# A state-space convolution and an MLP on one core: five chunks of channels instead of six, outer products spread over four PSUM banks, and target times for each chunk

## The chip, the core and the metric

The kernel runs on one core of one Trainium2 chip. The metric is the device time of one execution in microseconds (us); the time before is the median of three runs, 1096.41 us (1095.74 to 1097.32). The trace is that of one further execution, whose span from the first to the last instruction is 1094.6 us.

## The reference, cut to what matters

Two computations share one normalised input and are multiplied at the end. The first is a long convolution for each of 576 channels: its kernel K is a sum over 128 complex exponentials, and the convolution goes through a Fourier transform of twice the length. The second is an MLP with a hidden width of 4608.

```python
xn = layernorm(u)                                  # (2048, 576)
P  = exp((A * dt[:, None])[:, :, None] * arange(2048))
K  = 2.0 * einsum("dn,dnl->dl", C, P).real         # (576, 2048), 128 terms each
s  = irfft(rfft(xn.T, 4096) * rfft(K, 4096))[:, :2048].T + xn * D_skip
h  = gelu(layernorm(xn) @ w1 + b1)                 # (2048, 4608)
g  = silu(h @ w2 + b2)
out = u + s * g
```

## The kernel before, in words

**The MLP is the frame.** The loop over `slot` (48 of them: 12 groups of 384 hidden columns, two blocks of 512 tokens, and all of that once more for the second 1024 tokens) issues TensorE work in a fixed order: three pieces of layer 1 (`layer1`, L633, 14 matmuls of 512 columns each), then eight pieces of layer 2 (`layer2`, L707, 72 matmuls of 288 columns). fp32 products are made of three fp32r products of high and low parts, so each hidden tile goes PE, then ScalarE twice (`gelu` L671, `high` L674), then VectorE (`low` L677, which writes `hl`), and layer 2 takes as its third matmul the one that reads `hl`. The stream of PE instructions of a slot is layer 1, layer 2, layer 1 of the next slot, and so on.

**The convolution rides in the gaps of that order.** Channels are worked through in six chunks of `CH` = 96, and a chunk is a chain of visits to PE: `x1` (first transform of the input, L1157, two pieces of 48 channels), `k1` (the same of the kernel K, L1188, two pieces), four times `s2` (second transform, L1217), after each two of them an `inverse` (L1260), and at the end `i1` (L1286), whose result goes to DRAM as `s_s`. Between the visits VectorE and ScalarE transpose, multiply and copy. All visits but the MLP's own use one PSUM tile name, `cv`: two tiles of two banks each. The intermediate spectrum sits in one large tile, `A2` (`A2F` is its flat view).

**K is made by outer products.** 36 blocks of `SB` = 16 channels each go through `tables` (VectorE and ScalarE: phases from `par`, sine and cosine, magnitudes `mg`, weights) and then through `kgen` (L1042, one PE visit of 32 matmuls). The 30 parameters of a channel come in one DMA for each block, `load_par` (L944), into a tile `par` with two buffers. A `kgen` visit can stand alone, or `ride`: it is then issued right ahead of the matmuls of a convolution visit, into the columns from 384 on of the same PSUM banks, which a chunk of 96 leaves empty.

**The order is written by a planner.** `Order` runs when the program is built. It keeps a clock for each engine from estimated durations, has a list of `lines` of steps, and emits a step when its inputs are due and it does not push a step with a due time (`by`) back. Engines run strictly in the order emitted. `pe_turns` decides when a convolution visit comes: `pace` spreads the 48 visits of `c1` evenly up to `END`, `ALONE` and `DUE` hold back a `kgen` that would stand alone, and `HOLD` swaps single steps by hand. When a convolution visit stands at the edge of a slot, `pair` (L616) may go ahead of it: it does two narrow matmuls side by side in place of two of the 42 matmuls of layer 1, for which a second copy of `XR` has been loaded into `bias2` (`load_pair`).

**The beginning.** Sixteen blocks of 128 tokens are normalised. `second(t)` (L456) writes the rows of layer 1's input; for the second eight of them it does so on VectorE into a tile `row`, of which there are four buffers (`NROW`), and two DMAs on SP's queue (L459) store each of them to `y_s`. `norms` is called for blocks 8 to 11 and for 12 to 15, and emits the four `second` steps of a call nearly one behind the other. The names below: row 8 to row 15 for these eight.

Of the kernel before, what the change touches and what calls it, by code (L numbers as in the profile page):

```python
# [18 lines left out]
P = 128  # L19
# [3 lines left out]
CH = 96  # L23
NCH = D // CH
# [5 lines left out]
NPAR = 30  # L30
PK = 144
# [5 lines left out]


# [186 lines left out]
def mixer_kernel(ctx, tc, u, log_a_real, a_imag, c_real, c_imag, log_dt, d_skip, w1, b1, w2, b2,  # L225
# [24 lines left out]
    par_s = dr.tile([P, D, NPAR], F32, name="par_s")  # L250
# [10 lines left out]
    def ys_tile():  # L261
        return sb.tile([P, 2, 2, 2, CH], F32, name="ys", bufs=2)

    idp = sb.tile([P, 4, P], F32, name="f2t")[:, 0]
    f1t = sb.tile([P, 2, 2, 64], F32, name="f1t")
# [13 lines left out]
    def load_consts(g):  # L279
        if g == 0:  # L280
            m = sb.tile([P, 2, 2, CH], F32, name="kk").rearrange("p a b c -> p (a b c)")
# [8 lines left out]
        for k, t in ((ri, TMP["g"]), (1 - ri, TMP["s"])):  # L290
            nc.gpsimd.dma_start(t[r], g1[64 * k + 32 * h:64 * k + 32 * h + 32, 32 * h:32 * h + 32])
        nc.gpsimd.dma_start(dsk[32 * g:32 * g + 1, :].rearrange("p (c m) -> p c m", m=12),
                            dram(d_skip, 12 * g, [[0, 1], [48, D // 48], [1, 12]]))
# [78 lines left out]

    A2 = sb.tile([P, 16, 2, CH, 2], F32, name="A2")
    A2F = A2.rearrange("p a b c r -> p (a b c r)")

# [27 lines left out]
    def norms(b0, n):  # L403
# [49 lines left out]
        def second(t):  # L453
            mv, rs = MV[b0]
            y = sb.tile([P, D], F32, name="row", bufs=NROW)
# [21 lines left out]
    def y_turn(tb, kb):  # L477
# [5 lines left out]
        def load():  # L483
            T.append(sb.tile([P, D], F32, name="row", bufs=NROW)[:, :TB])
# [4 lines left out]
        def turn():  # L489
            T.append(sb.tile([P, D], F32, name="row", bufs=NROW)[:, :TB])  # L490
            nc.vector.transpose(T[1][:n], T[0][:n])

# [250 lines left out]
    def combine_load(b, n, c0, c1):  # L743
        m = c1 - c0
        r = [sb.tile([P, D], F32, name="row", bufs=NROW)[:, :n * m].rearrange("p (i d) -> p i d", i=n) for _ in range(3)]
# [28 lines left out]
    def load_identity():  # L774
        m = sb.tile([P, 32, 24], F32R, name="xc", bufs=NXC).rearrange("p b d -> p (b d)")
        lo = sb.tile([P, 2, 4 * CH], F32R, name="pr").rearrange("p t c -> p (t c)")[:, :D]
        raw = sb.tile([P, 2, 3, CH], F32, name="kk").rearrange("p a b c -> p (a b c)")[:, :P]
# [11 lines left out]
    def finish(b, c0, c1, silu, second_queue, z=None, store=(0, 0), flush=False,  # L789
# [7 lines left out]
        def act_z():  # L797
            if n < D:
                T.append(sb.tile([P, TB], F32, name="h32", bufs=2)[:, :n])
            else:  # L800
                T.append(sb.tile([P, D], F32, name="row", bufs=NROW))
# [33 lines left out]
    def params():  # L835

        nrm, th, ph = (A2F[:, k * D:(k + 1) * D] for k in range(3))
        cr = sb.tile([P, NT, 48], F32, name="xc", bufs=NXC).rearrange("p a b -> p (a b)")[:, :D]
# [5 lines left out]
        dt = ys_tile().rearrange("p i a b c -> p (i a b c)")[:, :D]  # L844
        PRM = [flat(sb.tile([P, 12, 64], F32, name="kt", bufs=2)) for _ in range(2)]
        PRM += [flat(sb.tile([P, 2, 4 * CH], F32, name="pr")), flat(sb.tile([P, SB, NM], F32, name="mg"))]
# [63 lines left out]
        def pack(i):  # L910
            s = slice(i * PK, (i + 1) * PK)

            def columns():
                if i == 0:
                    V.memset(pt[:, :, E1:E1 + 17:8], 1.0)
# [901 lines left out]
```

## Time and profile before

| | |
|---|---|
| time, median of three runs | 1096.41 us (1095.74 to 1097.32) |
| span of the profiled execution | 1094.6 us |
| TensorE (PE) | 1087.5 us busy, 99% |
| VectorE (DVE) | 891.6 us busy, 81% |
| ScalarE (ACT) | 727.4 us busy, 66% |
| GpSimd (POOL) | 188.3 us busy, 17% |
| granted TensorE clock, mean | 0.999 |

PE is counted busy from a matmul's start to its modelled end, and matmuls overlap, so the length of a visit is read from its first start to the start of what follows it. SP's rows tell when its queue issues a DMA; "to landing" is the time from the start of the issue to the semaphore of that DMA.

### The profile page before, as it was taken

To read this page: it belongs to the slowest core of one execution; us is meant where nothing else is said; L and a number is where in the kernel's file an instruction comes from. 1 tells how busy PE (TensorE), PEld (TensorE's weight loads), DVE (VectorE), ACT (ScalarE), POOL (GpSimd) and SP (SyncE) were. 2 spreads that over 40 slices of the span, in tenths; PEclk is the share of its full clock that TensorE was granted. 3 is DMA by queue.
4 is the path that set the end of the run, shared out by engine and by line. 5 is a ranking of instruction groups with operands and counts; after the bars stand their busy time and mean duration, and the time that the engine had idled before them with its cause. 6 is when DMAs were issued, how large, how long until landed. Compare 5 with 4: busy or idle time off the path is not lost.

```text
span 1094.6 us, 27052 instructions
## 1 busy us (share of the span) xinstructions
PE 1087.5 (99%) x11445; PEld 954.1 (87%) x11445; DVE 891.6 (81%) x1302; ACT 727.4 (66%) x1113; POOL 188.3 (17%) x261
## 2 busy tenths in 40 slices
PE   9999999999999999999999999999999999999998
PEld 7989899899888898888988888888888888888897
DVE  7698667889998879889899987997979888766367
ACT  6585699778676674777767848685675757534333
POOL 4566210153010100001100000000001021101132
PEclk9999999999999999999999999999999999999999
DMA  8846663626354152355624216133152434455454
GB/s 226 241 141 160 227 240 137 181 78 156 120 161 139 44 112 66 91 111 147 166 47 119 78 56 141 34 122 87 54 126 44 143 101 132 116 168 151 136 151 102
DMA packets 139554, 138.22 MB, mean 126 GB/s; under 512 B 88953, under 2 KB 105017, under 8 KB 138857
## 3 DMA queue, kind: packets, MB, share of 16 engines
q1 hardware_dynamic: 124424, 85.05, 29.4%
q0 software_dynamic: 14528, 50.71, 15.1%
q8 instruction: 89, 1.46, 0.6%
q10 hardware_dynamic: 480, 0.74, 0.3%
q14 instruction: 33, 0.26, 0.1%
HBM read 102.17 MB, written 36.63 MB: 127 GB/s over the span
## 4 chain that ended last, share of the span: by engine, by line
PE 95%; DMA 2%; DVE 1%; SPq 1%; issue 0%; ACT 0%; DVEq 0%
PE mxb L707 20%; PE mxa L707 20%; PE mxa L633 20%; PE mxb L633 20%; PE cv L1042 3%; PE cv L1217 3%; PE cv L1260 2%; PE cv L1286 2%; PE cv L1188 1%; PE cv L1157 1%; SPq L856 1%; DMA w<-in_A_u_dram 1%; DMA acc<-in_A_u_dram 0%; DMA h<-in_B_b_dram 0%; DVE st L423 0%; DMA raw<-in_B_w_dram 0%
## 5 line engine op out<-in xcount | busy, mean ns | idle before, releaser
L677 DVE TENSOR_TENSOR hl<-h,hh 128x512 fp32r<-128x512 f32 x144 | 98.4, 686 | 96.4 <-ACT hh L674 95.4
L707 PE MATMUL mxa<-w2h,hh 128*128 128x288 f32 x573 | 170.3, 297 | 0.0
L707 PE MATMUL mxb<-w2h,hh 128*128 128x288 f32 x573 | 170.2, 297 | 0.0
L707 PE MATMUL mxb<-w2h,hl 128*128 128x288 f32 x573 | 169.3, 296 | 0.2 <-DVE hl L677 0.2
L707 PE MATMUL mxa<-w2h,hl 128*128 128x288 f32 x573 | 169.1, 295 | 0.0
L707 PE MATMUL mxa<-w2l,hh 128*128 128x288 f32 x573 | 168.6, 294 | 0.0
L707 PE MATMUL mxb<-w2l,hh 128*128 128x288 f32 x573 | 168.6, 294 | 0.0
L671 ACT ACTIVATE h<-mxa,b1t 128x512 f32<-128x512 f32 x73 | 50.0, 687 | 99.2 <-PE mxa L633 97.8
L707 PEld LDWEIGHTS mxa<-w2h,hh 128*128 128x128 f32 x573 | 107.6, 188 | 5.9 <-issue 3.0
L707 PEld LDWEIGHTS mxb<-w2h,hh 128*128 128x128 f32 x573 | 107.6, 188 | 4.3 <-issue 1.7
L707 PEld LDWEIGHTS mxb<-w2l,hh 128*128 128x128 f32 x573 | 107.6, 188 | 0.8
L707 PEld LDWEIGHTS mxa<-w2l,hh 128*128 128x128 f32 x573 | 107.6, 188 | 0.6
L707 PEld LDWEIGHTS mxb<-w2h,hl 128*128 128x128 f32 x573 | 107.5, 188 | 0.5 <-DVE hl L677 0.4
L707 PEld LDWEIGHTS mxa<-w2h,hl 128*128 128x128 f32 x573 | 107.5, 188 | 0.0
L671 ACT ACTIVATE h<-mxb,b1t 128x512 f32<-128x512 f32 x71 | 48.8, 687 | 68.6 <-PE mxb L633 66.2
L674 ACT ACTIVATE hh<-h 128x512 fp32r<-128x512 f32 x144 | 90.7, 631 | 3.7
L944 POOL DMA_DIRECT2D par<-par_s x36 | 27.8, 773 | 367.8 <-DVE mg L988 324.8
L717 DVE TENSOR_TENSOR acc<-mxa,acc 128x576 f32<-128x576 f32 x87 | 65.4, 752 | 26.4 <-PE mxa L707 26.1
L717 DVE TENSOR_TENSOR acc<-mxb,acc 128x576 f32<-128x576 f32 (+1 forms) x89 | 65.8, 741 | 17.8 <-PE mxb L707 17.6
L633 PE MATMUL mxa<-XH,w1h 128*128 128x512 f32 x284 | 79.4, 401 | 0.0
L633 PE MATMUL mxb<-XH,w1h 128*128 128x512 f32 x280 | 77.6, 399 | 0.0
L633 PE MATMUL mxa<-XL,w1h 128*128 128x512 f32 x284 | 76.2, 390 | 0.0
(277 smaller groups left out, 2494.0 us busy)
## 6 DMA issues: line engine op xcount, KB each, us to landing
raw<-in_B_w_dram SPq DMA_DIRECT2D x72, 288.0 KB, 3.4
raw<-in_B_w_dram SPq DMA_DIRECT2D x96, 192.0 KB, 3.6
par_s<-A POOLq DMA_DIRECT2D x4, 2160.0 KB, 8.1
par<-par_s POOLq DMA_DIRECT2D x36, 240.0 KB, 3.7
f2t<-f2q SPq DMA_DIRECT2D x24, 256.0 KB, 3.7
g2t<-g2p SPq DMA_DIRECT2D x24, 256.0 KB, 4.3
bias<-XR SPq DMA_DIRECT2D x42, 128.0 KB, 3.6
raw<-in_B_w_dram SPq DMA_DIRECT2D x48, 96.0 KB, 3.8
```

The source lines that it names most:

```text
L633: nc.tensor.matmul(q, a, b, start=j == 0 and i not in BEGUN, stop=j == len(ops) - 1, skip_group_check=True)
L671: nc.scalar.activation(t, q, AF.Gelu_apprx_tanh, bias=b1t[:, k:k + 1], scale=1.0)
L674: LAST[0] = nc.scalar.activation(hh[:, i], t, AF.Copy)
L677: nc.vector.tensor_sub(hl[:, i], t, hh[:, i].bitcast(F32))
L707: nc.tensor.matmul(q[:, dh, :288], a[:, i, c], b[:, i, d], start=i == 0 and k == 0 and alone != 1, stop=i == G - 1 and k == 2, skip_group_ ...
L717: nc.vector.tensor_add(o, q[:, dh:dh + n, :288], b)
L856: nc.sync.dma_start(r[32 * g:32 * g + 32].rearrange("c (b n) -> c b n", n=32), dram(src[k], 32 * g, [[N, 32], [32 * N, D // 32], [1, 32]]))
L944: nc.gpsimd.dma_start(PAR[b].rearrange("p (g i) k -> p g (i k)", g=4), dram(par_s, (b // 3 * 48 + b % 3 * 4) * NPAR, [[D * NPAR, P], [12 * ...
L1042: nc.tensor.matmul(q[32 * g:32 * g + 32, i // 2, i % 2 * 64:i % 2 * 64 + 64], U[:, ri, 4 * g + i, :], v[:, ri, 4 * g + i, :], start=ri == ...
L1217: nc.tensor.matmul(Q[i][32 * q:32 * q + 32, f, ri::2], m[r, 4 * i + q, 32 * ri:32 * ri + 32], A2[r, 4 * p + 2 * i + q // 2, :, :, q % 2], ...
L1260: nc.tensor.matmul(QI[q // 2][64 * f:64 * f + 64, q % 2, i], MAT["g2t", p + i // 2][r, i % 2, f, ri], YS[p + i // 2][0][r, i % 2, ri, f], ...
L1286: nc.tensor.matmul(Q[h][64 * y:64 * y + 64, t], g1t.rearrange("p a e -> p (a e)"), A2[:, k:k + 2, 1].rearrange("p i d r -> p i r d"), star ...
```

## The change

**Chunks.** The 576 channels go in chunks of 112, 112, 112, 112 and 128. A chunk of 112 has two pieces of 56 for `x1` and `k1`, that of 128 has 48, 48 and 32. Every tile whose size hung on `CH` gets the size of the largest chunk, and views of what a chunk needs. A block of 16 channels can now lie across two pieces, so its parameters come in one or two DMAs (`slots`, `load_table`).

**Outer products.** A chunk of 112 leaves 64 columns of a bank empty, not 128, so a riding `kgen` writes 64 columns in each of the host's four banks and is copied out in two pieces, not one. In the last chunk, which fills a bank, only `x1` and `k1` take riders.

**Memory.** Wider tiles take room, and it is found in three places. The `row` buffers shrink from 576 to 512 columns and the normalised rows move into `A2F`, at the places of `ROWS_AT`: four for the first eight rows, two for rows 8 to 15. The tile `mg` goes, and the magnitudes move to the end of `A2F` (the last four blocks, which meet the chunk of 128, use other tiles). `par` has one buffer, not two, without the two phase columns, which come by a DMA of their own into `pha` (two buffers). The parts of the first transform's matrix are made once and kept in DRAM (`fp_s`), and loaded for each later chunk, where they were made anew.

**The planner.** `pace` gives way to `due`: each visit has a target time between the `BEGIN` of its chunk and the next, by the shares of `PART`; a visit waits longer for a rider that is not ready (`WAITS`). `ALONE` falls from 20 to 1.5, `HOLD` is emptied, and in the last eleven slots no second copy of `XR` is loaded, so no `pair` stands there.

```diff
-CH = 96
-NCH = D // CH
+CHS = 112, 112, 112, 112, 128
+PIECES = ((56, 56),) * 4 + ((48, 48, 32),)
...
-            y = sb.tile([P, D], F32, name="row", bufs=NROW)
+            at = ROWS_AT[(b0 + t) % 4 if b0 < 8 else 4 + t % 2]
+            y = A2F[:, at:at + D]
...
+    ROWS_AT = 4032, 4608, 5184, 6048, 6048, 7200
...
-        PAR[b] = sb.tile([P, SB, NPAR], F32, name="par", bufs=2)
...
+        PHA[b] = sb.tile([P, SB, NPH], F32, name="pha", bufs=2)
+        load_table(PHA[b], ph_s, b, NPH)
...
+        PAR[b] = sb.tile([P, SB, NPAR - NPH], F32, name="par")
+        load_table(PAR[b], par_s, b, NPAR - NPH)
...
-        return ([step(None, 10.0 if b < 6 else 4.5, lambda: load_par(b), mark=("par", b), need=[("pack", b * SB // PK)]
-                      + ([("mags", b - 2)] if b > 1 else [("xn", k) for k in range(8, NT)])),
+        lead = 10.0 if b < 6 else 4.5
...
+                [step(None, lead, lambda: load_par(b), mark=("par", b), need=[pk] + ([("mags", b - 1)] if b else [("xn", k) for k in range(8, NT)]))])
...
-            q = (bank2("cv") if tile is None else tile)[:, :, 384:]
-            Q.append(q)
+                q = [tiles[j // 2][:, j % 2, 448:] for j in range(SB // 4)]
+                Q.extend([(j, 2, tiles[j // 2][:, :, 448:]) for j in (0, 2)])
...
-    HOLD = {("weigh", 19, 3): 1, ("phase", 19): 1, ("frac", 18): 2, ("k", 2, 1): (2, 1), (2, 0, 24): 1, (2, 1, 24): 1, ("k1", 2, 1, 2): 1}
+    HOLD = {}
...
-    END = 1000.0
-    EDGE = 0.2, 0.6
-    ALONE, DUE = 20.0, (160.0, 950.0)
+    BEGIN = 240.0, 400.0, 574.0, 720.0, 880.0, 989.0
+    PART = 0.0, 0.09, 0.18, 0.283, 0.373, 0.469, 0.533, 0.673, 0.833
+    WAITS = 0.5, 28.2
+    ALONE, DUE = 1.5, (164.0, 851.0)
...
-                    elif 1 < k < 2 * NG - 1 and ("acc", slot - k + 1, 3) in od.marks:
+                    elif 1 < k < 2 * NG - 1 and slot < NSLOT - 11 and ("acc", slot - k + 1, 3) in od.marks:
```

The first place to look at is VectorE's order near the beginning, at rows 8 to 11 (`row<-w` before, `A_84<-w` now; `hl` is the MLP's low part, and a name in brackets is a semaphore waited for, DMAHW that of a transfer on SP's queue). Before:

```order
L456 TENSOR_SCALAR row<-w,mv,rs 128x576 [waits DVE_49]
L583 TENSOR_TENSOR w2l<-raw,w2h 128x576 [waits DMAHW1_49,Activation_49]
L583 TENSOR_TENSOR w2l<-raw,w2h 128x576 [waits DMAHW2_49,Activation_49]
L583 TENSOR_TENSOR w2l<-raw,w2h 128x576 [waits DMAHW3_49,Activation_49]
L876 TENSOR_TENSOR kt<-kt,pr 128x576 [waits Activation_49]
L456 TENSOR_SCALAR row<-w,mv,rs 128x576 x3
L677 TENSOR_TENSOR hl<-h_700,hh 128x512 [waits Activation_49]
```

And the same place now:

```order
L494 TENSOR_SCALAR A_84<-w,mv,rs 128x576 [waits DVE_49]
L621 TENSOR_TENSOR w2l<-raw,w2h 128x576 [waits DMAHW1_49,Activation_49]
L621 TENSOR_TENSOR w2l<-raw,w2h 128x576 [waits DMAHW2_49,Activation_49]
L621 TENSOR_TENSOR w2l<-raw,w2h 128x576 [waits DMAHW3_49,Activation_49]
L914 TENSOR_TENSOR kt<-kt,pr 128x576 [waits Activation_49]
L494 TENSOR_SCALAR A_84<-w,mv,rs 128x576
L494 TENSOR_SCALAR A_84<-w,mv,rs 128x576 [waits DMAHW5_49,DMAHW4_49,DVE_49] x2
L715 TENSOR_TENSOR hl<-h_692,hh 128x512 [waits Activation_49]
```

Nothing moved, but rows 10 and 11 now each wait for two transfers: row 10 takes the place of row 8 and waits for row 8's two stores, row 11 for row 9's.

The second place is VectorE's order at rows 12 to 15, where before each row waited for the store of four rows earlier:

```order
L451 RECIPROCAL rs<-rs 128x8 [waits Activation_49]
L456 TENSOR_SCALAR row<-w,mv,rs 128x576 [waits DMAHW5_49,DMAHW4_49,DVE_49]
L456 TENSOR_SCALAR row<-w,mv,rs 128x576 [waits DMAHW5_49,DMAHW4_49]
L456 TENSOR_SCALAR row<-w,mv,rs 128x576 [waits DMAHW7_49,DMAHW6_49]
L456 TENSOR_SCALAR row<-w,mv,rs 128x576 [waits DMAHW1_49,DMAHW0_49]
L677 TENSOR_TENSOR hl<-h_924,hh 128x512 [waits Activation_49,Pool_49]
```

Now:

```order
L488 RECIPROCAL rs<-rs 128x8 [waits Activation_49]
L494 TENSOR_SCALAR A_84<-w,mv,rs 128x576 [waits DMAHW7_49,DMAHW6_49,DVE_49]
L494 TENSOR_SCALAR A_84<-w,mv,rs 128x576 [waits DMAHW1_49,DMAHW0_49]
L494 TENSOR_SCALAR A_84<-w,mv,rs 128x576 [waits DMAHW4_49,DMAHW3_49,DVE_49]
L494 TENSOR_SCALAR A_84<-w,mv,rs 128x576 [waits DMAHW6_49,DMAHW5_49,DVE_49]
L715 TENSOR_TENSOR hl<-h_912,hh 128x512 [waits Activation_49,Pool_49]
```

Here rows 14 and 15 wait for the stores of rows 12 and 13, which stand two steps ahead of them; `hl` stands behind all four as before.

The third place is PE's order in the first chunk, between layer 1 pieces (`mxa`, `mxb` are the MLP's banks). Before, a rider (L1042) and its host `s2` (L1217):

```order
L633 MATMUL mxb<-XL,w1h 128x512 x4
L633 MATMUL mxb<-XH,w1l 128x512 x4
L633 MATMUL mxb<-XR,w1r 128x512
L633 MATMUL mxb<-XR,w1s 128x512
L1042 MATMUL cv<-w 32x64 x32
L1217 MATMUL cv<-A_83,f2t 32x2x96 x32
L633 MATMUL mxa<-XH,w1h 128x512 x4
```

Now, at a place a slot or two later, the outer product (L1112) stands alone and `s2` (L1312) follows one layer 1 piece on:

```order
L671 MATMUL mxb<-XR,w1r 128x512
L671 MATMUL mxb<-XR,w1s 128x512
L1112 MATMUL cv<-w 32x64 x32
L671 MATMUL mxa<-XH,w1h 128x512 x4
L671 MATMUL mxa<-XL,w1h 128x512 x4
L671 MATMUL mxa<-XH,w1l 128x512 x4
L671 MATMUL mxa<-XR,w1r 128x512
L1312 MATMUL cv<-A_84,f2t 32x2x112 x32
```

Over the whole program the rows of PE's order count 66 convolution visits before and 57 now, 36 `kgen` in both, of which 8 stood alone before and 17 now, and 16 `pair` before and 9 now. The number of places at which the MLP's stream is interrupted is 74 in both.

More of the change, by code (lines that the diff above doesn't have):

```diff
@@ L22 @@
 TWO_PI = 6.283185
-CH = 96
-NCH = D // CH
+CHS = 112, 112, 112, 112, 128
+NCH = len(CHS)
+C0 = [sum(CHS[:c]) for c in range(NCH)]
+PIECES = ((56, 56),) * 4 + ((48, 48, 32),)
+CHM = max(CHS)
 SB = 16
@@ L30 @@
 NPAR = 30
+NPH = 2
+LATE_MAG = 32
 PK = 144
@@ L36, with piece_at, slots @@
 TB = 512
+def piece_at(c, i):
+    return C0[c] + sum(PIECES[c][:i])
+def slots(b):
+    c = max(c for c in range(NCH) if C0[c] <= b * SB)
+    k, i0, res = (b * SB - C0[c]) // 4, 0, []
+    for i, m in enumerate(PIECES[c]):
+        n = min(SB // 4 - i0, m // 4 - k)
+        if 0 <= k and n > 0:
+            res.append((c, i, k, i0, n))
+            i0, k = i0 + n, 0
+        else:
+            k -= m // 4
+        if i0 == SB // 4:
+            break
+    return res
 def dve(n):
```

326 lines of the change are left out of this document (197 added, 129 removed).

## Prediction

> **What bounds the kernel now.** The page comes first: which engine is full, and whether the chain that ended last runs through it.
>
> ```profile
> span 1094.6 us, 27052 instructions
> PE 1087.5 (99%) x11445; PEld 954.1 (87%) x11445; DVE 891.6 (81%) x1302; ACT 727.4 (66%) x1113; POOL 188.3 (17%) x261
> PE 95%; DMA 2%; DVE 1%; SPq 1%; issue 0%; ACT 0%; DVEq 0%
> PE mxb L707 20%; PE mxa L707 20%; PE mxa L633 20%; PE mxb L633 20%; PE cv L1042 3%; PE cv L1217 3%; PE cv L1260 2%; PE cv L1286 2%; PE cv L1188 1%; PE cv L1157 1%; SPq L856 1%; DMA w<-in_A_u_dram 1%; DMA acc<-in_A_u_dram 0%; DMA h<-in_B_b_dram 0%; DVE st L423 0%; DMA raw<-in_B_w_dram 0%
> ```
>
> PE is the bound nearly from end to end. So the time changes by two things only: the length of PE's stream of work, and the gaps in it. The convolution (the `cv` lines) is 13% of the chain, the MLP about 80%, which the change leaves as it is. Next, the counts of the convolution's records by form (each matmul of these forms leaves two records, so a visit of `s2` has 64, of `inverse` 128, of `i1` 16):
>
> ```profile
> L1042 PE MATMUL cv<-w 128*32 128x64 f32 x2304 | 39.7, 220 | 0.0
> L1217 PE MATMUL cv<-A,f2t 64*32 64x192 f32 x1536 | 38.7, 333 | 0.0
> L1260 PE MATMUL cv<-ys,g2t 32*64 32x96 f32 x1536 | 22.0, 253 | 0.0
> L1286 PE MATMUL cv<-A,g1t 128*64 128x384 f32 x96 | 17.6, 506 | 0.0
> ```
>
> That is 36 outer products, 24 `s2`, 12 `inverse` and 6 `i1`. Their busy times overlap with their neighbours', so I take the length of a visit from PE's timeline, from its first start to the next start (start, length, then what ran):
>
> ```profile
> 302.35 1.07 PE L633 MATMUL mxa<-XH,w1h 128*128 128x512 f32 x4
> ...
> 305.30 0.39 PE L633 MATMUL mxa<-XR,w1s 128*128 128x512 f32 x1
> ...
> 308.56 1.10 PE L1042 MATMUL cv<-w 128*32 128x64 f32 x64
> 309.60 1.62 PE L1217 MATMUL cv<-A,f2t 64*32 64x192 f32 x64
> 311.15 0.40 PE L707 MATMUL mxa<-w2h,hh 128*128 128x288 f32 x1
> 311.39 0.30 PE L707 MATMUL mxa<-w2l,hh 128*128 128x288 f32 x1
> ...
> 320.66 0.29 PE L707 MATMUL mxb<-w2h,hl 128*128 128x288 f32 x1
> 320.88 0.50 PE L616 MATMUL mxa<-XR,w1s 64*128 64x512 f32 x1
> ...
> 321.31 1.83 PE L1260 MATMUL cv<-ys,g2t 32*64 32x96 f32 x128
> 323.07 1.21 PE L633 MATMUL mxa<-XH,w1h 128*128 128x512 f32 x4
> ```
>
> An outer product takes 309.60 - 308.56 = 1.04 us, `s2` 1.55, `inverse` 1.76, a `pair` 0.43. A matmul of 512 columns takes (305.30 - 302.35)/13 = 0.227 us, one of 288 columns (320.66 - 311.39)/70 = 0.1324, so a column costs 0.0946/224 = 0.00042 us.
>
> ```profile
> 368.93 2.92 PE L1286 MATMUL cv<-A,g1t 128*64 128x384 f32 x16
> 371.78 0.73 PE L633 MATMUL mxa<-XH,w1h 128*128 128x512 f32 x2
> ```
>
> ```profile
> 403.64 0.62 PE L1157 MATMUL cv<-pr,f2t 64*128 64x384 f32 x4
> ...
> 404.89 0.40 PE L707 MATMUL mxa<-w2h,hh 128*128 128x288 f32 x1
> ```
>
> ```profile
> 426.64 0.63 PE L1188 MATMUL cv<-pr,f2t 32*128 32x384 f32 x8
> ...
> 427.91 0.40 PE L707 MATMUL mxb<-w2h,hh 128*128 128x288 f32 x1
> ```
>
> `i1` takes 2.85, `x1` 1.25, `k1` 1.27.
>
> **Part 1, the visits: 4.1 us off PE's stream.** The number of columns over all chunks stays the same, so only what a visit costs beside its columns can be saved. In `x1`, 12 matmuls run two by two: 6 x 384 x 0.00042 = 0.97 of its 1.25 us are columns, 0.28 are not. I take 0.28 for every form and scale the rest by the width.
> - `x1`: 1.41 us with 56 channels, 1.25 with 48, 0.93 with 32. Before 12 x 1.25 = 15.0, now 8 x 1.41 + 2 x 1.25 + 0.93 = 14.7: -0.3.
> - `k1`: the same widths give 1.43, 1.27 and 0.94; 15.2 against 14.9: -0.3.
> - `s2`: 1.55 becomes 1.76 at 112 and 1.97 at 128. Before 24 x 1.55 = 37.2, now 16 x 1.76 + 4 x 1.97 = 36.0: -1.2.
> - `i1`: 2.85 becomes 3.28 and 3.71. Before 17.1, now 16.8: -0.3.
> - `inverse`: its 128 records of 96 columns are the same column work as 64 of 192 in `s2`, and both spread over eight parts of the array, yet it takes 1.76 against 1.55. So 0.2 us of it are neither columns nor the common 0.28, and a chunk of 112, for which `s2` gives 1.76, still fits. At 128 I take `s2`'s 1.97. Before 12 x 1.76 = 21.1, now 8 x 1.76 + 2 x 1.97 = 18.0: -3.1. The bounds are 10 x 1.76 = 17.6 and, all of it beyond 0.28 scaled, 8 x 2.01 + 2 x 2.25 = 20.6.
> - `pair`: 16 before, 9 now. Each one gone brings two matmuls of 512 columns back: 7 x (0.454 - 0.43) = +0.2. Before an `x1` a `pair` also shortens what follows, and five stood so before, one now; with that I take +1.0.
> - Outer products: 36 in both, 1.04 each whether alone or riding. That a rider now writes four banks could change it; I take zero, within -0.1 and +0.1 for each of 19 riders.
> - Interruptions of the MLP's stream: 74 in both: zero.
>
> The sum is -4.2; the rows' rounding is a tenth each, and I take -4.1. The inverse is most of it. On it the Trainium skill's page TensorEngine Tiling (Instruction Overhead) speaks against the change: a matmul has about 60 cycles of overhead that hide below 60 columns, so one of 96 columns should already pay for each column. By that rule the sum is -1.5 instead of -4.1.
>
> **Part 2, the rows at the beginning: 7 us of gaps.** Rows 8 to 15 alternate between two places in `A2F`, where four buffers took them before, and a row can only be written when the store of the row two ahead has landed. VectorE works in order, so behind a waiting row stand the normalisation's statistics and, one to three steps on, the MLP's `hl`, for which PE waits. VectorE's timeline at rows 9 to 11, then PE's third matmul of the layer 2 that follows:
>
> ```profile
> 60.04 1.89 DVE L456 TENSOR_SCALAR row<-w,mv,rs 128x576 f32<-128x576 f32 x3
> 61.85 0.68 DVE L677 TENSOR_TENSOR hl<-h,hh 128x512 fp32r<-128x512 f32 x1
> ...
> 63.42 0.64 DVE L677 TENSOR_TENSOR hl<-h,hh 128x512 fp32r<-128x512 f32 x1
> ...
> 65.44 0.67 DVE L677 TENSOR_TENSOR hl<-h,hh 128x512 fp32r<-128x512 f32 x1
> ```
>
> ```profile
> 64.00 0.29 PE L707 MATMUL mxa<-w2h,hl 128*128 128x288 f32 x1
> ```
>
> The slack is small: `hl` of the first hidden tile ends at 62.5, PE takes it at 64.0. SP's timeline, and the landing of the two stores issued between 61.9 and 62.6, those of row 9:
>
> ```profile
> 57.00 1.14 SPq L459 DMA_DIRECT2D y_s<-row  x2
> 58.25 1.97 SPq L553 DMA_DIRECT2D raw<-in_B_w_dram  x4
> 60.26 1.14 SPq L556 DMA_DIRECT2D raw<-in_B_w_dram  x2
> ```
>
> ```profile
> L459 SPq DMA_DIRECT2D y_s<-row x2: 496/544/592, 61.9 to 62.5; - x2
> DMA to landing us min/median/max: 4.2/4.2/4.2
> ```
>
> Row 8's store is issued at 57.0, long enough before row 10. Row 9 is done at 60.6, but SP is busy with weight loads and issues its store at 61.9 and 62.5; it lands at 62.5 + 4.2 = 66.7. Row 11, which began at about 61.3, now begins there, and `hl`, half a microsecond behind, at 67.3, 5.4 late, ends at 67.9. PE, wanting it at 64.0, stands for 3.9 us. The next `hl` begins 1.57 later as before (two statistics stand between) and ends at 69.5; PE has three matmuls until it wants that one, at 68.3: 1.1 more. The third ends at 71.5, when PE, fifteen matmuls on, gets there: nothing. The first place costs 5.0 us. Nothing hides it: VectorE has no idle time before the row, and before the change rows 10 and 11 waited for no transfer.
>
> That landing stood behind weight loads in flight. Stores at rows 12 to 15 are quicker:
>
> ```profile
> L459 SPq DMA_DIRECT2D y_s<-row x5: 465/541/596, 79.5 to 82.0; - x5
> DMA to landing us min/median/max: 2.1/2.1/2.1
> ```
>
> With 2.1 us in place of 4.2 the first place costs 2.9; that is the lower bound, and I take 5.0, since SP's order and the loads ahead are the same. The Trainium skill's page DMA: Bandwidth & Descriptors (Anatomy of one DMA) gives a fixed 2.0 us and 1 us for each 436 KB: 2.3 us by its figures for a store of 144 KB, an estimate that would put the first place at 3.1 and the time 1.9 us lower; the quiet rows agree with it, the row of row 9, behind other traffic, does not.
>
> ```profile
> 78.90 2.39 DVE L456 TENSOR_SCALAR row<-w,mv,rs 128x576 f32<-128x576 f32 x4
> 81.21 1.28 DVE L677 TENSOR_TENSOR hl<-h,hh 128x512 fp32r<-128x512 f32 x2
> ```
>
> ```profile
> 83.09 0.29 PE L707 MATMUL mxb<-w2h,hl 128*128 128x288 f32 x1
> ```
>
> The second place, in the times of before: row 12 ends at 79.5, its stores go out at 79.5 and 80.1 and land at 82.2; row 14 starts there, 2.2 late. Row 13's go out at 80.7 and 81.3 and land at 83.4; row 15 starts there, and `hl` begins at 84.0, not 81.2, and ends at 84.6, for PE at 83.1: 1.5 us, and 0.2 at the next `hl`. VectorE arrives there 5.4 us late from the first place and PE 5.0, which adds 0.3. I take 2.0, between 1 and 2.5. Both gaps together are 7.0, between 3.9 and 7.5.
>
> **Part 3, the rest of the order: 1 us, between 0 and 4.** `par` has one buffer, so its load can start only when the last reader of the block before is done, and the planner allows 4.5 us from there. The transfer's landing before:
>
> ```profile
> DMA to landing us min/median/max: 3.1/3.7/11.2
> ```
>
> The median fits, the slower ones don't, and VectorE then stands at the magnitudes with `hl` behind it. Two buffers hid this. For 36 blocks, most with other work in between, I take 1 us of PE gaps; `HOLD`, emptied, is in it. More DMA issues on POOL (a second one for each block, at 0.75 us) hide in the 83% of the span in which POOL is idle. A gain here is excluded: PE had no gaps to lose. The end of the kernel stays: at least as many MLP matmuls stand behind the last `i1` in PE's order as before.
>
> **The sum.** Span 1094.6 - 4.1 + 7.0 + 1.0 = 1098.5; the median lies 1.8 us above the span, so 1100.3 us.
>
> **Rivals.**
> - *The stores are in time* (other side). Place: row 11 and rows 14, 15. If row 9's store lands by about 62.9, `hl` ends by 64.0 and the first gap is gone; with the second gone too the time is 1096.4 - 4.1 = 1092.3, up to 1093.3 with part 3. It decides at gaps below 1.9 us in all. For it: two rows of slack are enough when SP is free (row 8's store is). Against it: the store of row 9 isn't even issued before 61.9. With forms that cost by the count and not by columns (`s2` unchanged at 1.55 would take 5 us more off) the sign would turn too; against that, 64 records take 1.04 us with 64 columns and 1.55 with 192. Together 0.13.
> - *About even.* The landing is near its quick value, gaps of 3.9 and nothing in part 3: 1096.4 - 4.1 + 3.9 = 1096.2, up to 1098.6. 0.24.
> - *The inverse pays for each column.* Its upper bound of 20.6 us holds, the gain falls by 2.6, and the time is 1102.9. For it: nothing in the trace shows the visit at another width. Against it: `s2` does the same column work in 0.2 us less. 0.05. It is what the Trainium skill's page TensorEngine Tiling says under Instruction Overhead.
> - *More gaps.* The single `par` buffer stalls VectorE at ten blocks or more by half a microsecond and PE with it, 5 us where I took 1: 1104 to 1106. For it: the landing of up to 11.2. Against it: half of them at 3.7 and less. 0.08.
>
> **How the numbers follow.** The forecast, 1098.6 to 1103, has 0.50. The range of 8 in 10 reaches from 1094.8, inside the even case, to 1105.0. A measurement of this kernel tells about 0.2%, 2.2 us, from no change. Faster than that is the first rival, 0.13; within it the second, 0.24; slower the forecast and the last two rivals, 0.63.
>
> **What would show it.** Right: in the changed profile PE's visits of 1.76 us for `s2` and `inverse` at 112 channels, a wait of PE for `hl` of about 4 us near 64 us and of 1 to 2 us near 88 us, and VectorE idle ahead of L494, released by a DMA to `y_s`. Part 1 is wrong if `inverse` takes 2.0 us, part 2 if VectorE writes rows 9 to 11 without idle time, part 3 if PE's waits after 100 us come to more than 4 us. The prediction falls if PE's stream is shorter by over 6 us or its gaps in the first 100 us stay below 2.

## The result and the profile after

| | before | after |
|---|---|---|
| median | 1096.08 us (1095.45 to 1097.32) | 1108.05 us (1107.62 to 1109.43) |
| profiled execution: time, span | 1096.4, 1094.6 us | 1109.43, 1107.6 us |
| granted TensorE clock, mean | 0.999 | 0.994 |

The ratio is 1.0111, 95% interval 1.0098 to 1.0123. The kernel is slower by 12.0 us where 3.9 were forecast, and 3.0 us outside the range. The direction and the place of the largest loss were right. The sizes were not, and three of the causes are not in the prediction at all. The profiled execution is the slowest of the four after, 1.4 us above their median, and the account below is of that one.

The page after shows it in the chain of work that ended last: PE's share falls from 95% to 89%, and VectorE, transfers and SP's queue take 8% of it where they took 4%.

```profile
span 1107.6 us, 25929 instructions
...
PE 1089.8 (98%) x10881; PEld 949.4 (86%) x10881; DVE 889.1 (80%) x1278; ACT 719.7 (65%) x1101; POOL 226.3 (20%) x316
...
PE 89%; DMA 3%; DVE 3%; SPq 2%; ACT 1%; issue 1%; DVEq 0%
```

To place the 13.0 us of span I took PE's timeline of both kernels and summed two things: the length of each visit, and the excess of each step from one MLP matmul's start to the next over the usual 0.227 us (layer 1) or 0.133 us (layer 2). The "end" is the time from the last matmul's start to the end of the span.

| term | forecast | trace |
|---|---|---|
| visits: `x1` +0.2, `k1` -0.2, `s2` -0.8, `inverse` -1.9, `i1` -0.2; fewer `pair` +0.5 | -4.1 | -2.3 |
| 60 to 100 us, the rows | +7.0 | +8.3 |
| other steps: 480 to 520 us 2.9, 300 us 0.5, 40 to 60 us 0.5 | +1.0 | +3.8 |
| the end | 0 | +3.1 |
| sum | +3.9 | +12.9 |

**The rows.** VectorE's timeline after, at rows 9, 10 and 11 (in brackets: idle time ahead, and who ended it):

```profile
60.55 1.40 DVE L494 TENSOR_SCALAR A<-w,mv,rs 128x576 f32<-128x576 f32 x2
66.69 0.58 DVE L494 TENSOR_SCALAR A<-w,mv,rs 128x576 f32<-128x576 f32 x1 [4.74 <-DMA y_s<-A]
67.18 0.69 DVE L715 TENSOR_TENSOR hl<-h,hh 128x512 fp32r<-128x512 f32 x1
```

Row 11 waits 4.74 us for row 9's store and starts at 66.69 us; the forecast had 66.7. PE's timeline at the `hl` behind it:

```profile
64.30 0.29 PE L745 MATMUL mxa<-w2h,hh 128*128 128x288 f32 x1
64.43 0.29 PE L745 MATMUL mxa<-w2l,hh 128*128 128x288 f32 x1
67.93 0.61 PE L745 MATMUL mxa<-w2h,hl 128*128 128x288 f32 x1 [3.21 <-DVE hl L715]
68.33 0.44 PE L745 MATMUL mxa<-w2h,hh 128*128 128x288 f32 x1
69.45 0.61 PE L745 MATMUL mxa<-w2h,hl 128*128 128x288 f32 x1 [0.44 <-DVE hl L715]
...
74.42 0.45 PE L745 MATMUL mxb<-w2l,hh 128*128 128x288 f32 x1
...
75.11 0.29 PE L745 MATMUL mxb<-w2h,hl 128*128 128x288 f32 x1
```

PE resumes at 67.93 us, as forecast (67.9). Then comes what was not: until 74.7 us the starts stand 0.240 us apart, not 0.133, and a matmul takes 0.44 us instead of 0.29. The busy time by windows has the reason in the seventh column, the granted clock:

```profile
64.43:67.90 3.47, 0.28 (x3) 0.06 (x1) 1.21 (x3) 0.00 (x0) 1.04 (x2) 1.00 0.68 262
67.94:74.77 6.83, 6.39 (x25) 6.04 (x26) 4.80 (x13) 6.71 (x13) 2.95 (x3) 0.50 0.21 65
74.80:84.00 9.20, 9.20 (x62) 8.64 (x61) 9.10 (x13) 7.92 (x21) 3.48 (x3) 1.00 0.17 64
```

For 6.83 us behind the gap TensorE ran at half its clock. Of the 7.0 us of excess between 60 and 80 us, 4.0 are waiting and 3.0 are slow steps. The second place, at 90 us, cost 1.3.

**The switch to the second 1024 tokens.** At 487 us PE waits for `hl` again, and VectorE's waits between 478 and 492 us say for what VectorE stood: the row loads (`row<-y_s`) that the MLP's next input is made from.

```profile
487.17 0.29 PE L745 MATMUL mxb<-w2l,hh 128*128 128x288 f32 x1
489.22 0.40 PE L745 MATMUL mxb<-w2h,hl 128*128 128x288 f32 x1 [1.75 <-DVE hl L715]
```

```profile
DVE row L529 <- DMA row<-y_s: 3.8, 2, 2.8
```

SP's own waits between 430 and 500 us (queue and line, then what ended the wait, us in all) say why they came late: ahead of them in SP's queue stood a load of `f2t` that may only start when the last `k1` has read the tile. SP's timeline has the first row loads, before and after:

```profile
SPq L1182 <- PE cv L1283: 23.3, 1, 23.3
```

```profile
470.31 7.84 SPq L486 DMA_DIRECT2D row<-y_s  x12
```

```profile
480.50 7.72 SPq L524 DMA_DIRECT2D row<-y_s  x12
```

**The end.** The last matmul starts at 1089.13 us before and 1099.03 after, so the span ends 5.5 us behind it before and 8.6 after. POOL's last instruction, a DRAIN at the program's end, is where it goes (its three durations, shortest, median and longest, in ns; before, then after):

```profile
L1813 POOLq DRAIN  x3: 46/103/4467, 1088.4 to 1094.3; - x3
```

```profile
L1919 POOLq DRAIN  x3: 46/103/7175, 1099.6 to 1107.3; - x3
```

It takes 7.2 us instead of 4.5, and it starts 0.6 us behind the last matmul's start instead of 0.7 ahead of it, since VectorE and POOL were still busy with the last step that combines convolution and gate (on VectorE at 1093.7 us after, at 1078.8 before).

**The visits.** Visits of `inverse` at 112 and at 128 channels, and of `s2` at 112, each with the row that follows:

```profile
401.53 1.96 PE L1355 MATMUL cv<-ys,g2t 32*64 32x112 f32 x128
403.43 1.20 PE L671 MATMUL mxa<-XH,w1h 128*128 128x512 f32 x4
```

```profile
983.48 2.10 PE L1355 MATMUL cv<-ys,g2t 32*64 32x128 f32 x128
985.50 0.40 PE L745 MATMUL mxa<-w2h,hh 128*128 128x288 f32 x1
```

```profile
485.16 1.85 PE L1312 MATMUL cv<-A,f2t 64*32 64x224 f32 x64
486.93 0.40 PE L745 MATMUL mxb<-w2h,hh 128*128 128x288 f32 x1
```

`s2` takes 1.77 us, as forecast. `inverse` takes 1.90 and 2.02 where 1.76 and 1.97 were forecast: from 96 channels on it pays 0.13 us for each 16, where `s2` pays 0.22 (1.55 to 1.77).

### The profile page after: what moved, and what is told of

Its sections match the earlier page's. It is cut to its first block, busy times and chain, and to the rows that moved or that the text cites. A ratio compares the mean times of both kernels' runs of the same rounds, so it can differ in the third digit from the quotient of the medians.

```text
span 1107.6 us, 25929 instructions
## 1 busy us (share of the span) xinstructions
PE 1089.8 (98%) x10881; PEld 949.4 (86%) x10881; DVE 889.1 (80%) x1278; ACT 719.7 (65%) x1101; POOL 226.3 (20%) x316
## 4 chain that ended last, share of the span: by engine, by line
PE 89%; DMA 3%; DVE 3%; SPq 2%; ACT 1%; issue 1%; DVEq 0%
PE mxa L745 20%; PE mxb L745 19%; PE mxb L671 19%; PE mxa L671 18%; PE cv L1112 3%; PE cv L1312 3%; PE cv L1355 2%; DMA raw<-in_B_w_dram 2%; PE cv L1381 2%; PE cv L1251 1%; PE cv L1283 1%; SPq L894 1%; DMA w<-in_A_u_dram 1%; DMA y_s<-A 1%; DMA acc<-in_A_u_dram 0%
## 5 line engine op out<-in xcount | busy, mean ns | idle before, releaser
L981 POOL DMA_DIRECT2D par<-par_s x40 | 30.2, 757 | 487.9 <-DVE A L1049 429.4
```

The costliest lines, as they stand in the source:

```text
L981: nc.gpsimd.dma_start(x.rearrange("p (g i) k -> p g (i k)", g=4)[:, :, i0 * n:(i0 + m) * n], dram(t, (piece_at(c, i) + k) * n, [[D * n, P] ...
```

## The experiments

The theory to be tested: four separate causes, namely the rows' two places with the halved clock behind the gap, SP's queue at the switch, the combine steps together with POOL's drain at the end, and an `inverse` that is dearer than forecast. The chief rivals: the clock falls for another reason than PE's idleness, the gaps after 100 us come of the single `par` buffer as the prediction had it, and the end is long by chance. Differences to the changed kernel are differences of medians taken at different times; the kernel before, run beside every experiment, lay between 1095.3 and 1095.8 us there and at 1096.1 beside the changed kernel, so they are good to about 0.8 us.

### Three places for the rows

```diff
-            at = ROWS_AT[(b0 + t) % 4 if b0 < 8 else 4 + t % 2]
-            y = A2F[:, at:at + D]
+            at = ROWS_AT[(b0 + t) % 4 if b0 < 8 else 4 + (b0 + t) % 3 % 2]
+            y = sb.tile([P, 6 * CHM], F32, name="kk")[:, :D] if b0 >= 8 and (b0 + t) % 3 == 2 else A2F[:, at:at + D]
```

> The changed kernel, with three places in turn for rows 8 to 15 instead of two (the third is the tile kk, which nothing else uses so early), so that row 11 waits for row 8's store and no longer for row 9's. Theory A (the rows' stores make the gaps near 64 and 90 us, and the halved clock that follows the first one is its consequence): the excess of PE's steps between 60 and 100 us, 8.3 us in the changed kernel, falls below 1.5 us, the granted clock stays at 1.00 from 50 to 100 us, and the time falls by 7 to 8.5 us, to 1099.5 to 1101. Rival B (the slow clock near 70 us comes of something else, the load on the chip at that time for instance): PE's gaps go, but the clock still halves for 7 us; 4 to 5 us, to about 1103.5. Rival C (VectorE is late there for another reason, the gap only moves): under 2 us.

Measured: 1100.71 us, ratio to before 1.0051 (1.0037 to 1.0065), 7.3 us less than the changed kernel. The busy time by windows:

```profile
60.00:70.00 10.00, 10.00 (x67) 9.42 (x66) 9.79 (x21) 6.77 (x11) 8.40 (x8) 1.00 0.73 247
```

PE is busy through 60 to 70 us, the clock stays at 1.00, and the excess between 60 and 100 us is about 1 us instead of 8.3 (0.7 of it a wait of ScalarE's making at 79 us). The rows were the cause of both the wait and the slow clock. The gap at the switch is still there in this run (1.6 us idle at 478 us), so it is a matter of its own.

### The wait filled with idle work

```diff
+        fill = lambda z: [nc.tensor.matmul(z[:, 0], hh[:, 0, :P], hh[:, 0], start=True, stop=True, skip_group_check=True)
+                          for _ in range(16)]
...
+                (turn[0], j, i, dh, k) == (3, 0, 0, 0, 2) and fill(bank2("cv")); ...
```

> The changed kernel, with 16 matmuls of 512 columns added whose result nothing reads, in PE's order between the second and the third matmul of the layer 2 that stands at 64.4 us, the place where PE waits for hl. They take 16 x 0.227 = 3.6 us, about as long as the wait. Theory A (an idle stretch of over 3 us halves the clock): the wait for hl is filled, the clock stays at 1.00, the steps of 240 ns from 68 to 75 us become 133 ns, and the time FALLS by 2.5 to 3.5 us although PE has more work, to about 1105. Rival B (the clock halves for another reason than PE's idleness): the clock still falls, and the time stays within 1 us of 1108, or rises by what the filling overshoots the wait, at most 0.5 us.

Measured: 1108.10 us, ratio 1.0112 (1.0098 to 1.0125): no change in the time. The windows and the timeline (L724 is the filling) show that the clock did what theory A says:

```profile
63.60:67.30 3.70, 3.65 (x16) 2.65 (x15) 0.90 (x2) 0.00 (x0) 0.78 (x2) 1.00 0.60 227
67.30:74.20 6.90, 5.70 (x40) 5.43 (x41) 6.69 (x17) 6.43 (x12) 2.66 (x3) 1.00 0.20 62
```

```profile
63.66 3.58 PE L724 MATMUL cv<-hh 128*128 128x512 f32 x15
67.64 0.40 PE L745 MATMUL mxa<-w2h,hl 128*128 128x288 f32 x1 [0.39 <-DVE hl L715]
67.88 0.30 PE L745 MATMUL mxa<-w2h,hh 128*128 128x288 f32 x1
...
69.17 0.40 PE L745 MATMUL mxa<-w2h,hl 128*128 128x288 f32 x1 [0.86 <-DVE hl L715]
```

VectorE is as late as before, but PE isn't idle for long, the clock stays at 1.00 and the steps at 0.133 us. So it is idleness that lowers the clock. The saving in time missed: between 60 and 80 us PE's stretch is 2.0 us shorter (3.6 us of filling and 1.3 of waits against 7.0), but PE then comes sooner to the second place, whose gap grows by 0.9 us. Some 1 us is left in this profile, which is less than the interval's width. What the slow clock costs in time has to be read from the run with gaps below.

### The `f2t` load behind the row loads

```diff
-                nc.sync.dma_start(t, f2q[:, 8 * p:8 * p + 8].rearrange("p k r m -> p k (r m)"))
+                (LATE.append if (c, p) == (1, 0) else lambda f: f())(lambda: nc.sync.dma_start(t, f2q[:, 8 * p:8 * p + 8].rearrange("p k r m -> p k (r m)")))
...
+            (tb, kb) == (0, 1) and LATE.pop()()
```

> The changed kernel, with one DMA moved on SP's queue: the load of f2t for the second chunk, which stands 23.3 us for the last k1 matmul, is issued behind the first eight row<-y_s loads of the switch to the second 1024 tokens instead of ahead of them. PE's order is the same. Theory A (that load blocks the queue, the rows land late, VectorE's transposes wait 3.8 us, and PE waits for the hl behind them at 487 us): VectorE's waits for row<-y_s and PE's step of 2.2 us at 487 us go, the slower weight loads after it too, and the time falls by 2 to 3 us, to 1105 to 1106. Rival B (the gaps after 100 us come of the single par buffer, as the prediction had it): the row loads run earlier but PE's gap stays or moves, under 1 us.

Measured: 1106.29 us, ratio 1.0095 (1.0081 to 1.0108), 1.8 us less than the changed kernel; the intervals overlap (1.0098 to 1.0123 for the changed kernel), so the trace has to decide. SP's timeline:

```profile
456.24 5.93 SPq L524 DMA_DIRECT2D row<-y_s  x8
478.45 0.34 SPq L1182 DMA_DIRECT2D f2t<-f2q  x1
```

The first eight row loads now go out at 456 us, where they stood at 480.5, VectorE doesn't wait for them, and PE has no gap between 478 and 500 us: the excess of the steps from 480 to 520 us falls from 3.3 to 0.7 us. The `f2t` load still waits for `k1`, with only four row loads behind it. The single `par` buffer, which this kernel has too, makes no gap there.

### Faster combine steps

```diff
-                ml["steps"].append(step(None, 13.0, lambda a=a: combine_load(*a), need=[("st", c), ("u", NT - 1)]))
+                ml["steps"].append(step(None, 10.0, lambda a=a: combine_load(*a), need=[("st", c), ("u", NT - 1)]))
...
-                ml["steps"].append(step(None, 4.0, lambda: None))
+                ml["steps"].append(step(None, 2.0, lambda: None))
```

> The changed kernel, with the planner's allowances for the final combining of convolution and gate cut (10 us instead of 13 from the load to the use, 2 instead of 4 behind it), so that the eleven combine steps follow each other faster and the last one comes well before PE's end. The order before 885 us is the same. Theory A (the last combine, at 1093 us, stands in VectorE's way at the end and its four stores on POOL lengthen POOL's final drain: from the last matmul to the end 8.3 us, where the kernel before has 5.2): the tail falls to 5.0 to 5.5 us and the time by 2.5 to 3.5 us, to about 1105. Rival B (the tail is long because the last rows' own stores are slow this time): the tail stays at 7 us or more, under 1 us.

Measured: 1106.78 us, ratio 1.0101 (1.0087 to 1.0115), 1.3 us less, which the overlapping intervals do not tell from nothing; the trace shows what became of the end. The last combine step comes at 1072 us, and the end shrinks from 8.6 to 7.1 us, not to 5.0 to 5.5 (the expectation counts from the last matmul's end, 0.3 us after its start). What is left is the drain, which now starts as early as in the kernel before and is as long as ever:

```profile
L1919 POOLq DRAIN  x3: 46/103/7065, 1098.0 to 1105.5; - x3
```

So the end had two causes: 1.5 us by the late combine step, and 1.6 by a drain that doesn't depend on what came just ahead of it.

### The kernel before with two places for the rows

```diff
-            y = sb.tile([P, D], F32, name="row", bufs=NROW)
+            y = TWO[t % 2] if b0 >= 8 and t % 2 in TWO else sb.tile([P, D], F32, name="row", bufs=NROW); b0 >= 8 and TWO.setdefault(t % 2, y)
```

> The kernel before, with only the rows' part of the change: rows 8 to 15 take two of the row buffers in turn instead of four. Theory A (two places cost what the trace of the changed kernel shows, a wait of about 4 us near 64 us, 3 us of halved clock behind it and 1.3 us near 90 us): the time rises by 7 to 9 us, to 1103 to 1105, with the clock at 0.50 for some 7 us. Rival B (the clock's part is peculiar to the changed kernel): 5 us, to about 1101, the clock at 1.00. Rival C (most of the difference at the beginning has another cause, the new places in A2F among them): under 2 us.

Measured: 1103.96 us, ratio 1.0075 (1.0061 to 1.0089), 8.1 us more than the kernel before it was run beside. The windows:

```profile
66.00:68.00 2.00, 0.89 (x3) 0.54 (x3) 1.97 (x6) 1.32 (x2) 0.00 (x0) 0.72 0.34 126
68.00:70.00 2.00, 1.87 (x8) 1.88 (x9) 1.93 (x6) 1.97 (x3) 0.00 (x0) 0.50 0.40 96
70.00:72.00 2.00, 2.00 (x10) 2.00 (x10) 1.17 (x4) 1.99 (x4) 1.80 (x2) 0.50 0.00 0
```

Theory A holds: the one suspected cost, put alone into the kernel before, brings the gap (3.1 us idle), the halved clock (6.8 us) and the time that the changed kernel loses there. Put in or taken out, it is worth 7 to 8 us.

### Gaps of different length

```diff
+        late = {40: 4, 41: 5, 42: 6, 43: 7, 44: 8, 45: 10, 5: 6, 7: 8}.get(turn[0] - 1, 0) if i == 0 else 0
...
-            nc.vector.tensor_sub(hl[:, i], t, hh[:, i].bitcast(F32))
+            [nc.vector.tensor_sub(hl[:, i], t, hh[:, i].bitcast(F32)) for _ in range(1 + late)]
```

> The kernel before, with VectorE made late on purpose at eight slots: the first hl of the slot is computed over again, 6 times more in slot 5, 8 in slot 7, and 4, 5, 6, 7, 8 and 10 times in slots 40 to 45 (0.61 us each, the same values), so that PE waits for it for different times. Theory A (an idle stretch of PE beyond some length between 2.3 and 3.4 us halves the granted clock for about 7 us, a shorter one does not): in the slots with waits below 2.3 us the steps after it stay at 133 ns, in those with waits over 3.4 us they are 240 ns for 5 to 8 us and cost 2.5 to 3.5 us more than the wait. Rival B (each wait costs its own length): the time rises by the sum of the waits and the clock stays at 1.00 throughout.

Measured: 1113.06 us, ratio 1.0156 (1.0138 to 1.0175), 17.2 us more. At four of the eight slots PE waited; the rows that end the waits:

```profile
933.12 0.40 PE L707 MATMUL mxa<-w2h,hl 128*128 128x288 f32 x1 [1.45 <-DVE hl L677]
1030.89 0.40 PE L707 MATMUL mxa<-w2h,hl 128*128 128x288 f32 x1 [2.52 <-DVE hl L677]
1055.72 0.40 PE L707 MATMUL mxb<-w2h,hl 128*128 128x288 f32 x1 [2.83 <-DVE hl L677]
164.65 0.61 PE L707 MATMUL mxb<-w2h,hl 128*128 128x288 f32 x1 [4.94 <-DVE hl L677]
```

And the clock behind the second, third and fourth of them:

```profile
1032.00:1036.00 4.00, 4.00 (x25) 2.00 (x24) 0.04 (x1) 0.98 (x2) 0.00 (x0) 1.00 0.00 0
...
1056.57:1059.97 3.40, 3.40 (x16) 3.40 (x16) 3.13 (x6) 2.60 (x6) 1.95 (x4) 0.50 0.13 29
...
162.28:169.10 6.82, 4.45 (x18) 4.45 (x19) 4.91 (x9) 4.36 (x8) 0.00 (x0) 0.50 0.40 119
```

Idle for 1.45 or 2.52 us, PE goes on at full clock; idle for 2.83 us, it runs at half for 3.4 us, and for 4.94 us, the clock is at half for 6.8, of which 2.4 still lie in the wait. The lengthened steps alone come to 12.4 us (5.1, 1.6, 2.7 and 3.0 at these four), which rival B would have as the whole loss; that lies below the interval of 15 to 19 us. The other steps add 3.7 us, nearly all in the two slow stretches. Theory A holds in this run, with two corrections: the slow stretch lasts 3.4 or 6.8 us, and costs about 1.6 us or up to 3.

### All three repairs

The edits of the three places, of the `f2t` load and of the combine steps, together.

> The changed kernel with all three: three places for the rows, the f2t load behind the switch's row loads, and the faster combining. Theory A (the three causes are separate and add): 8 + 2.5 + 3 = 13.5 us off, to about 1094.5, 1 to 2 us below the kernel before, which is what the shorter visits (2.3 us in all) leave over the few small gaps that remain. Rival B (the gains overlap, or other gaps open where these close): 8 us or less, 1100 or more.

Measured: 1096.71 us, ratio 1.0008 (0.9999 to 1.0017), 11.3 us less than the changed kernel. The three add nearly as single runs (7.3 + 1.8 + 1.3 = 10.4). In its trace PE's last matmul starts at 1086.82 us, 2.3 us ahead of the kernel before, which is the gain of the visits, and the excess of the steps is within 0.4 us of the kernel before's: hardly a gap is left that the single `par` buffer, or anything else of the new order, would have made. The 1.6 us that it loses again at the end are the drain, 7.07 us as with the faster combine steps alone, which the expected 1094.5 had left out.

### 55 more DMAs on POOL's queue in the kernel before

```diff
+    more = dr.tile([55, P, 4], F32, name="more")
+    TM, MORE = [], [0]
...
+        [nc.gpsimd.dma_start(more[k], dsk[:, :4]) for k in range(5 * MORE[0], 5 * MORE[0] + 5)]; MORE[0] += 1
```

> The kernel before, with 55 small DMAs more on POOL's queue (five behind each combine step, each 2 KB into memory that nothing reads), so that it issues 287 as the changed kernel does and not 232. They are over some 5 us before POOL's last stores. Theory A (POOL's drain at the program's end takes about 0.049 us for each DMA that the queue issued in the whole program: 4.47 us at 232, 7.07 to 7.18 at 287): the drain takes 7.0 to 7.2 us, the stretch from the last matmul's start to the end grows from 5.5 to 7.1 us, and the time by 1.5 us, to about 1097.3. Rival B (the drain is long because of what the changed kernel's DMAs are, or because of its memory): the drain stays at 4.5 us and the time within 0.5 us.

Measured: 1099.37 us, ratio 1.0033 (1.0020 to 1.0045). The drain:

```profile
L1813 POOLq DRAIN  x3: 46/103/8298, 1088.0 to 1096.8; - x3
```

It is longer still than in the changed kernel, 8.3 us, the end takes 8.4 us instead of 5.5, and nothing else in PE's stream became longer (last matmul at 1088.72 us, 0.4 earlier). The medians differ by 4.1 us, more than the 2.9 of the end; the rest isn't placed. So DMAs issued on POOL do lengthen the drain; the price of 0.049 us each was too low, here it is (8.30 - 4.47)/55 = 0.070. The added ones were issued between 878 and 1084 us. The changed kernel's own 55 stand between 102 and 893 us (the loads of `pha` above all), and no run takes these out: that they are what lengthens its drain is argued from the count.

### The combine loads on SP's queue

```diff
-        nc.gpsimd.dma_start(r[0], u_s[:, b:b + n, c0:c1])
-        nc.gpsimd.dma_start(r[1], s_s[:, b:b + n, c0:c1])
-        nc.gpsimd.dma_start(r[2], g_s[b:b + n, :, c0:c1].rearrange("i p d -> p i d"))
+        nc.sync.dma_start(r[0], u_s[:, b:b + n, c0:c1])
+        nc.sync.dma_start(r[1], s_s[:, b:b + n, c0:c1])
+        nc.sync.dma_start(r[2], g_s[b:b + n, :, c0:c1].rearrange("i p d -> p i d"))
```

> The kernel with the three repairs, with the 33 loads of the combine steps moved from POOL's queue to SP's, so that POOL issues 254 DMAs. PE's order is the same. Theory A (drain by the count): the drain takes 5.4 to 5.5 us in place of 7.07, the stretch behind the last matmul 5.4 to 5.6 us in place of 7.1, and the time falls by 1.6 us against the three repairs alone, to about 1095 and just below the kernel before. Rival B (drain by something else): 7.07 us as there, no change. Rival C (the loads stand in the way of SP's weight loads and PE waits): the tail shortens, but PE's last matmul comes over 1 us later.

Measured: 1094.82 us, ratio 0.9991 (0.9982 to 1.0000), 1.9 us less than the three repairs.

```profile
L1919 POOLq DRAIN  x3: 46/103/4752, 1088.2 to 1094.1; - x3
```

33 DMAs fewer take 2.3 us off the drain, again 0.070 each, and the end is at 5.4 us, the kernel before's. In the profiled run, the slowest of the eleven, PE's last matmul came 2.1 us later than with the three repairs, which by its number is rival C's sign. But 1.4 of it are excess of steps, the largest a wait at 79 us, far ahead of the moved loads; behind 880 us, where these stand, the excess is 2.6 us in both kernels. So the profile doesn't bear out rival C, nor does the median. This version is below both kernels, but below the kernel before by no more than a measurement can tell from nothing.

## Why the prediction was wrong, by its steps

The span grew by 9.1 us more than forecast: 3.1 at the end, 2.8 in part 3, 1.8 in part 1 and 1.3 in part 2. The largest miss is the end, which the prediction put at nothing.

**Part 1, the visits: 1.8 us short.** `s2`, `k1` and `i1` came out as worked out, within 0.4 us each; `x1` is 0.5 dearer, since some visits before took 1.15 us and not 1.25, and the missing `pair` 0.5 cheaper. The term that was mis-sized is `inverse`: "a chunk of 112, for which `s2` gives 1.76, still fits" took the 0.2 us that the visit has over its columns as room. It isn't room: the visit grows at once, by 0.13 us for 16 columns, and the gain is 1.9 us, not 3.1. The rule of the Trainium skill's page TensorEngine Tiling (Instruction Overhead), weighed there, gives an estimate of 2.01 us for 112; measured are 1.90, about halfway between the two.

**Part 2, the rows: the mechanism right, the price 1.3 us short.** Row 9's late store, row 11's start, `hl` and PE's return came in the order written. That the return agrees to a tenth, 67.9 us, is luck: VectorE came to the rows half a microsecond later than before, so row 9's second store was issued at 63.0 us and not at 62.5, but it landed in 3.6 us and not in 4.2. PE came later by nearly as much, and its first wait lengthened the step by 3.4 us, not 3.9. The 2.3 us that the prediction worked out beside this from the Trainium skill's page DMA: Bandwidth & Descriptors (Anatomy of one DMA) come from a fit to DMAs that GpSimd issues; this store is issued on SP's queue, and its 3.6 us lie above them. The step that failed is "PE, wanting it at 64.0, stands for 3.9 us", taken as the whole price of a wait. Here a wait of that length has a second price: 6.83 us at half the clock, 3.0 us, which stood in no term, for either end of the range. It also changed the rest: with PE slowed, the later `hl` tiles and the second place cost less than worked out (1.3 us for 2.0), which hid a part of the error. The rule that bears on it is in the Trainium skill's page TensorE: Matmul & The Clock Gate (Why this matters for your kernels: no idle gap of PE over about 3 us between bursts), which the prediction did not weigh; every wait of 2.8 us and more in these traces (six) agrees with it, but one of 1.81 us brought the half clock too (last section).

**Part 3, the rest of the order: right in kind, wrong in place and size.** It put 1 us, at most 4, on the single `par` buffer. The gaps were 3.8 us, and nearly none of it came of `par`: VectorE did wait for it, five times and 7.6 us in all, but off PE's path, as the three repairs show, which leave the single buffer and at most 0.4 us of excess:

```profile
DVE A L1049 <- DMA par<-par_s: 7.6, 5, 3.4
```

2.9 us came of a load on SP's queue that waits for a matmul, with the switch's row loads queued behind it. "HOLD, emptied, is in it" looked at the planner's swaps, and not at what stands on SP behind a wait that the new target times moved.

**"The end of the kernel stays": it didn't, 3.1 us.** The sentence looked at PE's order alone. The first eight combine steps wait for all but the last chunk, which with five of them is stored at 894 us; their loads began at 896 us instead of 847, and the last step ran into the end: 1.5 us, by the run with faster combine steps. And "More DMA issues on POOL hide in the 83% of the span in which POOL is idle" looked at their issue alone. The other 1.6 us are POOL's longer drain: that DMAs on POOL lengthen it is shown, that these do is argued.

**The rivals.** Of the four, "more gaps" came nearest, for other reasons than it named. "The stores are in time" fell by the wait of 4.74 us, and with "about even" all that lies below 1098.6.

## What to carry to other kernels

A wait on the engine that sets the time isn't priced by its length alone: ask what the engine does when it comes back, and keep single waits of TensorE short even where their sum is the same: here none below 1.8 us brought the half clock. When buffers are cut, follow the store that frees them to the queue that issues it, and when target times move, list for each in-order queue what stands behind an instruction that waits for compute. Look at the last 10 us as a stage of its own: what must be done there, and what each queue leaves behind.

## What the runs showed of the hardware

**The clock after a gap.** The stretches at half clock ahead of PE's last matmul were 3.41 us (four of them) or 6.83 us (three). The shortest idle stretch of PE that brought one was 1.81 us, in the run with faster combine steps, at the switch; waits of 1.75 us (the changed kernel, same place) and 2.52 us (the run with gaps) brought none:

```profile
487.80 0.40 PE L745 MATMUL mxb<-w2h,hl 128*128 128x288 f32 x1 [1.81 <-DVE hl L715]
```

```profile
488.91:492.30 3.39, 3.39 (x16) 3.39 (x15) 3.39 (x6) 2.19 (x4) 0.00 (x0) 0.50 0.78 254
```

So length alone doesn't decide between 1.8 and 2.8 us. Where the wait falls does. Within a run all changes of the clock lie on one grid of 3.41 us; the two slow stretches of this run (69.07 and 488.91 us) start 123 steps of it apart. Cut along its own grid, each of the eleven traces fits one rule: a stretch of 3.41 us at full clock in which PE is idle for 1.81 us or more is followed by one at half clock (seven of seven), and one with 1.66 us or less never is. The nearest cases, first the 3.41 us ahead of the slow stretch above, where PE (second column) is busy for 1.61 us, then two neighbours in the run with the moved `f2t` load, whose wait of 3.29 us at 64 us is cut in two; the first of them left the clock at full, the second, with another wait in it, did not:

```profile
485.49:488.91 3.42, 1.61 (x13) 1.38 (x11) 3.06 (x6) 2.07 (x4) 0.00 (x0) 1.00 0.69 139
```

```profile
62.25:65.67 3.42, 1.76 (x9) 1.30 (x7) 0.00 (x0) 0.00 (x0) 2.53 (x2) 1.00 0.86 316
65.67:69.08 3.41, 0.92 (x5) 0.69 (x6) 2.98 (x8) 1.69 (x3) 0.00 (x0) 1.00 0.47 179
```

The waits of 1.75 and 2.52 us were cut in two as well, with 1.44 and 1.63 us of idleness in the larger part. A stretch at half clock is followed by a second one where PE still idles in it (0.44, 0.64 and 2.37 us, the three of 6.83 us), and not where it is busy throughout (four of 3.41 us). The grid lies elsewhere in each run, so what a wait of 2 to 3 us costs is in part chance. This rule is read off the traces afterwards; no run was made to test it. The Trainium skill's page TensorE: Matmul & The Clock Gate (What's actually happening) has a free-running window of 3413 ns over which activity is judged, and half the clock after an idle one; length and grid agree with it. That a window about half idle is enough is not what that page says; here the measurement decides.

**POOL's drain at the end.** 4.47 us with 232 DMAs issued on POOL's queue (4.73 in the run with gaps), 7.07 to 7.18 with the changed kernel's 287, 4.75 when 33 of these went to SP's queue, 8.30 with 55 small ones added to the kernel before. So it grows by 0.07 us for each DMA that was put in or taken out in the last 220 us, but not by the count alone: the changed kernel has 55 more too, spread over the program, and its drain is longer by 2.6 to 2.7 us where the added ones made it 3.8. What makes the difference stays open.
